# A routed two-block kernel: the search for the next expert visits TensorE at other places among the current expert's products

## The chip, the cores and the metric

One core of one Trainium2 chip. The metric is the device time of the whole kernel in microseconds. Three runs of the kernel before gave 707.58 us as median (704.78 to 709.69), and its profiled execution has a span of 709.6 us.

## What is computed

Two blocks follow each other. The first is linear attention with a norm: for every batch and head `kv = k^T v`, `out = q kv`, divided by its root mean square and scaled by `g_norm`. The second routes the 4608 tokens (512 wide) to 8 experts, 576 tokens each, and applies the expert's two-layer network:

```python
logits = x @ w_gate                       # 4608 x 8
order = np.argsort(-logits.flatten())
for idx in order:                         # the highest logit first
    tok, e = idx // E, idx % E
    if assigned[tok] >= 0 or counts[e] >= cap: continue
    assigned[tok] = e; counts[e] += 1
for e in range(E):
    h = np.maximum(x[assigned == e] @ w1[e], 0.0)    # 512 -> 1024
    out[assigned == e] = h @ w2[e]                   # 1024 -> 512
```

The greedy loop fills the experts one after the other. The kernel finds which expert fills next, and with which tokens, by a search for a threshold among the logits; expert t of the kernel, counted from 0 to 7, is the one that fills as number t.

## The kernel before

**Stages.** The attention takes the first part of the span and leaves its result in DRAM (`x_dram`). Then the first expert's tokens are searched with nothing beside it, and from 180.3 us on the eight experts' products run on TensorE one expert after the other, the last ending at 699 us. While expert t is multiplied, the search for a later expert is woven in between.

**One expert's products** (`layers`, L763). 64 fp32 matmuls of the first layer (`h_ps`, L798), then 56 of the second layer in seven products of eight (`y_ps`, L847; a Strassen-like scheme whose operand sums `tw` L779 and `sh` L789 GpSimd makes), then 8 for the last 64 tokens (L858). I call the place after k of these 128 matmuls "place k of expert t". VectorE makes six additions of these products (L818) and a last one for the 64 tokens (L866).

**One search** (`control`, L703) is a chain that goes to and fro between TensorE and VectorE. I name it after the expert it finds: search 1 to search 7, the last of which has no counting to do (`rest`, L598).

- seven counting steps (`threshold`, L468): TensorE counts with nine small matmuls (`n_ps`, L478) how many tokens lie over each of 32 candidate thresholds; VectorE finds the interval (L484 to L524), makes 32 new candidates (L271) and compares all tokens with them (`over`, L266), which the next count reads. The first count reads an `over` made right after the choice.
- the assignment (`assign`, L533): VectorE makes `sums` (L551), TensorE adds them up over the partitions (`all_ps`, L555), VectorE works out which tokens are taken. `here` (L561, L563) is part of it.
- the list (`fetch`, L627): VectorE makes `along` (L640), TensorE `a_ps` (L643), VectorE `since` (L652), TensorE `s_ps` (L656), and VectorE the row numbers `ids` (L668) with which GpSimd gathers the tokens from DRAM in five indirect transfers (`xg`, L673). VectorE then makes the output rows (L688 to L699).
- the choice (`choice`, L238): VectorE finds every token's best expert among those still open (L245 to L259), as the start of the next search.

**The turn** (`turn`, L723): VectorE scales the gathered tokens (`xs`, L733), TensorE transposes them (`t_ps`, L747), ScalarE writes `xt`, the next expert's input.

**What sets the order.** TensorE, VectorE and ScalarE run in the order in which the code records their instructions; GpSimd's is fixed too (`in_order`, L614). A search is a generator: each `yield` gives the time, in nominal microseconds of products, that TensorE is to spend on products before the search's next part is recorded. `layers` yields the nominal time of every matmul (0.487, 0.38, 0.858 for a pair), the main loop subtracts it, and when the wait is used up the next part is recorded there:

```python
                    wait -= used
                    while wait <= 0 and search():
                        pass
```

The number thus does not make an engine wait; it sets how many matmuls stand in TensorE's queue between one visit and the next. If VectorE is not ready when TensorE reaches the visit, TensorE stands still. Three other things steer the order: `search()` (L884) stops when two experts' weights are asked for ahead; at the first of the places marked `None` in `layers` (L839) a list that is still missing is recorded at once; and the turn begins 5.0 nominal microseconds (`hold`) after the list is recorded, its transposes standing at the marked places.

Of the kernel before, what the change touches and what calls it, by code (L numbers as in the profile page):

```python
# [25 lines left out]
def kernel(  # L26
# [16 lines left out]
    E, _, F = moe_w1.shape  # L43
# [93 lines left out]
    def small(nm, w=1, dt=FT):  # L137
        return asg.tile([P, w], dt, name=nm, tag="s_" + nm, bufs=2)
# [99 lines left out]
    def choice(c0=None, c1=GC):  # L238


        cs = slice(c0 or 0, c1)
        n = cs.stop - cs.start
        m, cm, cd = (mx, code_mx, code) if c0 is not None else (small_ps[k] for k in ("mx", "code_mx", "code"))
        if c0 is None:
            nc.vector.tensor_tensor(wl, lg, bc_e(small_ps["shut"]), op=AL.add)  # L245
        else:
            nc.vector.tensor_scalar(lg[:, :, cs], in0=lg[:, :, cs], scalar1=bound, scalar2=bottom,
                                    op0=AL.min, op1=AL.max)
        w = wl if c0 is None else lg
        nc.vector.tensor_reduce(m[:, cs], w[:, :, cs].rearrange("p e c -> p c e"), axis=AXX, op=AL.max)  # L250
        yield
        nc.vector.tensor_tensor(pick[:, :, cs], w[:, :, cs], bc_c(m[:, cs]), op=AL.is_ge)
        nc.vector.tensor_tensor(pick[:, :, cs], pick[:, :, cs], bc_e(cd, n), op=AL.mult)
        yield
        nc.vector.tensor_reduce(cm[:, cs], pick[:, :, cs].rearrange("p e c -> p c e"), axis=AXX, op=AL.max)
        yield
        nc.vector.tensor_tensor(best[:, :, cs], pick[:, :, cs], bc_c(cm[:, cs]), op=AL.is_equal)
        if c0 is None:
            nc.vector.tensor_tensor(mx, m, gone, op=AL.add)  # L259
# [5 lines left out]
    def compare(over, cand, c0=0, c1=GC):  # L265
        nc.vector.tensor_tensor(  # L266
            over[:, c0:c1], mx[:, c0:c1].rearrange("p (c o) -> p c o", o=1).to_broadcast([P, c1 - c0, NCAND]),
            cand[:, 1:NCAND + 1].rearrange("p (o n) -> p o n", o=1).to_broadcast([P, c1 - c0, NCAND]), op=AL.is_ge)

    def candidates(s, lo, cand):  # L270
        nc.vector.tensor_scalar(cand, in0=away[:, s], scalar1=lo, scalar2=None, op0=AL.add)  # L271
        return cand
# [170 lines left out]
    def bank(shape, nm):  # L443
        return psm.tile(shape, FT, name=nm, tag="c", bufs=1)
# [15 lines left out]
    def pieces():  # L460

        turn_of[0] += 1
        sm = small_ps["step"][:, turn_of[0] % 2]
        return sm[:, 0:2], sm[:, 2:]
# [3 lines left out]
    def threshold(t, over):  # L468

        lo, hi = bottom, top  # L470
        first, cand = t == 0, cand0
        for s in range(NSTEP):
            yield 4.6 if s > 0 else 0.4 if first else 2.0 if t == 1 else 4.0


            n_ps = bank([P, E, G], "n_ps")
            for c in range(0, GC, G):
                nc.tensor.matmul(n_ps, lhsT=over[:, c:c + G].rearrange("p c n -> p (c n)"),  # L478
                                 rhs=best[:, :, c:c + G],
                                 start=(c == 0), stop=(c == GC - G))  # L480
            need = goal[0:QP]
            for g in range(1, G):
                less = small("need", E)[0:QP]
                nc.vector.tensor_tensor(less, need, n_ps[g * QP:(g + 1) * QP, :, g], op=AL.subtract)  # L484
                need = less
            full = small("full", E)[0:QP]
            n_full = small("n_full")[0:QP]
            nc.vector.scalar_tensor_tensor(full, in0=n_ps[0:QP, :, 0], scalar=0.0, in1=need, op0=AL.add,
                                           op1=AL.is_ge, accum_out=n_full)
            if s + 1 < NSTEP:  # L490
                over = asg.tile([P, GC, NCAND], BF, name="over", tag="over", bufs=2)
            if first:
                ends = small("ends", 2)
                hi, lo = ends[:, 0:1], ends[:, 1:2]

                def pick_end(n):
                    at = small("at", NCAND + 1)
                    nc.vector.scalar_tensor_tensor(at, in0=row_f[:, 0:NCAND + 1], scalar=k_ps, in1=cand[:, n:NCAND + 1 + n],
                                                   op0=AL.is_equal, op1=AL.mult, accum_out=ends[:, 1 - n:2 - n])

                some = small("some_b", dt=BF)[0:QP]
                nc.vector.tensor_scalar(some, in0=n_full, scalar1=0.5, scalar2=None, op0=AL.is_gt)
                k_ps = psm.tile([P, 1], FT, name="k_ps", tag="h")
                nc.tensor.matmul(k_ps, lhsT=ones_b[0:QP, :], rhs=some, start=True, stop=True)
                pick_end(0)
                if s + 1 < NSTEP:
                    cand_next = small("cand", NCAND + 2)
                    compare(over, candidates(s + 1, lo, cand_next[:, 0:NCAND + 1]))
                pick_end(1)
                if s + 1 < NSTEP:  # L510
                    nc.vector.tensor_copy(cand_next[:, NCAND + 1:NCAND + 2], hi)
                    cand = cand_next
            else:

                some, some_t, kk = (small_ps[k][0:QP] for k in ("some", "some_t", "kk"))
                nc.vector.tensor_scalar(some, in0=n_full.to_broadcast([QP, 2 * QP]), scalar1=0.5, scalar2=None, op0=AL.is_gt)
                nc.vector.transpose(some_t[:, :, 0:QP], some.rearrange("p (t n) -> p t n", t=2))
                nc.vector.reduce_sum(out=kk, in_=some_t, axis=AXX)  # L520

                lo_was, (ends, cand_ps) = lo, pieces()
                for g in range(G):
                    nc.vector.tensor_scalar(ends[g * QP:(g + 1) * QP], in0=kk, scalar1=width[0:QP, s:s + 1],  # L524
                                            scalar2=lo_was[0:QP], op0=AL.mult, op1=AL.add)
                lo = ends[:, 1:2]
                if s + 1 < NSTEP:
                    compare(over, candidates(s + 1, lo, cand_ps))
                hi_was, hi = hi, small("hi")
                nc.vector.tensor_tensor(hi, ends[:, 0:1], hi_was, op=AL.min)  # L530
        return hi, lo

    def assign(t, ends):  # L533
# [15 lines left out]
        sums = small("sums", 2 * E, BF)  # L549
        with nc.allow_low_precision("counts of up to GC are exact in bf16"):  # L550
            nc.vector.reduce_sum(out=sums, in_=two.rearrange("p t e c -> p (t e) c"), axis=AXX)  # L551
        yield 5.4

        all_ps = bank([P, 3, E], "all_ps")
        nc.tensor.matmul(all_ps[:, 0], lhsT=ones_b, rhs=sums[:, 0:E], start=True, stop=True)  # L555
# [42 lines left out]
    def rest():  # L598
        which = small_ps["which"]
        nc.vector.tensor_reduce(which, code_left, axis=AXX, op=AL.max)  # L600
        index = small("index", dt=I32)
        nc.vector.tensor_scalar(index, in0=which, scalar1=-1.0, scalar2=float(E), op0=AL.mult, op1=AL.add)
        mine = small_ps["mine"]
        nc.vector.scalar_tensor_tensor(mine, in0=mx, scalar=NONE / 2, in1=small_ps["code_mx"], op0=AL.is_ge, op1=AL.mult)
        nc.vector.tensor_tensor(who, who, mine, op=AL.max)
        return which, index, lambda: None
# [20 lines left out]
    def fetch(t, which, index):  # L627
# [10 lines left out]
        nc.vector.tensor_scalar(own, in0=who, scalar1=which, scalar2=None, op0=AL.is_equal)  # L638
        along = small("along", GC, BF)
        nc.vector.tensor_tensor_scan(along, ones_b[:, 0:GC], own, 0.0, op0=AL.mult, op1=AL.add)  # L640
        yield 3.2 if t == 1 else 4.2 if t < E - 1 else 2.4
        a_ps = bank([P, GC + 1], "a_ps")
        nc.tensor.matmul(a_ps[:, 0:1], lhsT=before, rhs=along[:, GC - 1:GC], start=True, stop=True)  # L643
        nc.tensor.matmul(a_ps[:, 1:GC + 1], lhsT=fall, rhs=along, start=True, stop=True)
# [5 lines left out]
            nc.vector.tensor_scalar(since, in0=slot_f, scalar1=a_ps[:, 0:1], scalar2=None, op0=AL.is_ge)  # L650
        else:
            nc.vector.tensor_tensor(since, slot_f, a_ps[:, 0:1].to_broadcast([P, NB * P]), op=AL.is_ge)  # L652
        yield 1.6
        s_ps = bank([P, NB, GC + 3], "s_ps")
        for n in range(NB):
            nc.tensor.matmul(s_ps[:, n], lhsT=since[:, n * P:(n + 1) * P], rhs=kn, start=True, stop=True)  # L656
# [24 lines left out]
                              reason="TensorE waits for the tokens")  # L681
        if t > 0:
            yield "tokens"
            yield 1.5

        up = asg.tile([P, NB, 2, GC], FT, name="up", tag="up")
        for n in range(2):
# [15 lines left out]
    def control(t):  # L703

        if t < E - 1:
            which, index, later = yield from assign(t, (yield from threshold(t, compared.pop(t))))
        else:
            which, index, later = rest()
        if t > 0:
            yield "weights"  # L710
        yield from fetch(t, which, index)
        later()

        pause = None if t == 0 else 0.9
        if t + 1 < E:
            for _ in choice():
                yield pause
            yield pause
        if t + 1 < E - 1:
            compared[t + 1] = asg.tile([P, GC, NCAND], BF, name="over", tag="over", bufs=2)  # L720
            compare(compared[t + 1], candidates(0, bottom, pieces()[1]))
# [147 lines left out]
    with tc.manual_schedule(engines={PE, DVE, ACTE}):  # L869
# [3 lines left out]
        first = turn(0)  # L873
# [76 lines left out]
```

## Time and profile before

| what | value |
| --- | --- |
| device time, median of three | 707.58 us |
| TensorE busy, of the 709.6 us span | 616.8 us |
| VectorE busy | 443.3 us |
| GpSimd busy | 263.8 us |
| first expert's products begin, last expert's end | 180.3, 699 us |
| TensorE waiting for another engine between 205 us and the end | 9.3 us in 7 waits |

In a page of the profile, "busy" is the time an engine spent on instructions[...]. A row of the timeline gives the start, the time taken, the engine, the line, what is written from what, and in square brackets the idle time before it and the instruction whose end ended that idle time. A name such as `held_ps` stands for several small tiles that share one PSUM bank.

### The profile page before, as it was taken

How to read it: one execution, taken by the hardware profiler on the slowest of the kernel's cores; microseconds unless marked ns; L12 is line 12 of the kernel's file. 1: busy time of each engine (PE TensorE's matmuls, PEld its weight loads, DVE VectorE, ACT ScalarE, POOL GpSimd, SP SyncE). 2: the span in 40 equal slices, each digit the busy share in tenths (PEclk: the TensorE clock that was granted, in tenths of full speed). 3: DMA queues.
4: the chain of work that ended last, by engine and by line, in shares of the span. 5: the costliest groups of instructions: out<-in, count | busy, mean ns of one | idle time of the engine just before them, and what ended most of it. 6: DMA issues, size and time to landing. Idle time of an engine off the chain costs nothing.

```text
span 709.6 us, 13280 instructions
## 1 busy us (share of the span) xinstructions
PE 616.8 (87%) x5370; PEld 482.7 (68%) x5370; DVE 443.3 (62%) x1393; ACT 155.9 (22%) x315; POOL 263.8 (37%) x249
## 2 busy tenths in 40 slices
PE   3787788214999899989998999999899999999994
PEld 2566666212778677857885788678677867877782
DVE  4344656888687778888878779887887545020011
ACT  1454555300211121022102111121112022112100
POOL 0100011002342562438344632735263659226322
PEclk9988977555999999999999999999999999999998
DMA  8987889405303600531081053108013843001001
GB/s 283 316 278 237 278 297 351 177 0 184 129 1 103 251 26 1 205 137 38 6 306 67 1 180 132 68 1 312 28 41 127 293 165 106 0 30 38 0 1 67
DMA packets 41405, 93.41 MB, mean 132 GB/s; under 512 B 3456, under 2 KB 3456, under 8 KB 41344
## 3 DMA queue, kind: packets, MB, share of 16 engines
q1 hardware_dynamic: 34752, 72.49, 29.1%
q0 software_dynamic: 5888, 20.06, 8.1%
q8 instruction: 42, 0.69, 0.4%
q14 instruction: 19, 0.16, 0.1%
q10 hardware_dynamic: 704, 0.02, 0.1%
HBM read 72.50 MB, written 20.05 MB: 130 GB/s over the span
## 4 chain that ended last, share of the span: by engine, by line
PE 74%; DVE 13%; issue 6%; DMA 4%; ACT 1%; POOL 1%; POOLq 0%; ACTq 0%; DVEq 0%
PE h_ps L798 35%; PE y_ps L847 20%; PE o_ps L370 3%; PE qt_ps L301 3%; PE y_ps L858 3%; PE kv_ps L313 3%; PE t_ps L747 2%; DVE over L266 2%; DMA xg<-x_dram,ids 2%; PE n_ps L478 2%; DVE xs L733 1%; DMA gw<-in_moe_w_gate_dram 1%; PE warm_ps L625 1%; DVE need L484 1%; DVE held_ps L524 1%
## 5 line engine op out<-in xcount | busy, mean ns | idle before, releaser
L798 PE MATMUL h_ps<-xt,w_sb 128*128 128x288 f32 x1024 | 260.1, 410 | 0.8 <-ACT xt L750 0.8
L798 PEld LDWEIGHTS h_ps<-xt,w_sb 128*128 128x128 f32 x1024 | 190.6, 190 | 55.4 <-issue 5.7
L801 ACT ACTIVATE hid<-h_ps 128x288 f32<-128x288 f32 x128 | 52.6, 411 | 208.1 <-PE h_ps L798 208.1
L847 PE MATMUL y_ps<-tw,sh 128*128 128x256 f32 x384 | 86.5, 380 | 0.0
L847 PEld LDWEIGHTS y_ps<-tw,sh 128*128 128x128 f32 x384 | 72.0, 190 | 9.3
L789 POOL TENSOR_TENSOR sh<-hid 128x512 f32<-128x512 f32 x32 | 41.7, 1303 | 94.4 <-ACT hid L801 94.3
L673 POOL DMA_INDIRECT xg<-x_dram,ids x40 | 38.6, 964 | 82.8 <-DVE ids L668 35.8
L750 ACT ACTIVATE xt<-t_ps,g_col 128x512 f32<-128x512 f32 (+1 forms) x40 | 25.8, 645 | 161.6 <-PE t_ps L747 161.6
L847 PE MATMUL y_ps<-w_sb,hid 128*128 128x256 f32 x256 | 57.8, 381 | 0.0
L266 DVE TENSOR_TENSOR over<-mx,held_ps 128x1152 bf16<-128x1152 f32 x42 | 56.9, 1354 | 1.5
L818 DVE TENSOR_TENSOR y_sb<-y_ps,u 128x512 f32<-128x512 f32 x24 | 16.4, 684 | 63.8 <-PE y_ps L847 63.8
L756 POOL DMA_INDIRECT out_dram<-y_sb,outs x32 | 33.4, 1043 | 52.1 <-issue 36.7
L847 PEld LDWEIGHTS y_ps<-w_sb,hid 128*128 128x128 f32 x256 | 48.1, 190 | 6.6
L524 DVE TENSOR_SCALAR held_ps<-held_ps,width 32x2 f32<-32x2 f32 x144 | 41.3, 287 | 5.3
L779 POOL TENSOR_TENSOR tw<-w_sb 128x512 f32<-128x512 f32 x32 | 39.9, 1269 | 12.4 <-DMA w_sb<-in_moe_w_dram 12.3
L478 PEld LDWEIGHTS <-over 128*128 128x128 bf16 x441 | 17.5, 97 | 38.8 <-DVE over L266 27.5
L370 PE MATMUL o_ps<-kvx,qt 64*64 64x72 f32 x1152 | 32.9, 261 | 9.8 <-issue 9.2
L733 DVE TENSOR_TENSOR xs<-xg 128x512 f32<-128x512 f32 (+1 forms) x40 | 31.9, 809 | 14.7 <-DMA xg<-x_dram,ids 8.1
L478 PE MATMUL n_ps<-best,over 128*128 128x32 bf16 x441 | 19.3, 179 | 21.1 <-DVE over L266 19.2
L370 PEld LDWEIGHTS o_ps<-kvx,qt 64*64 64x64 f32 x1152 | 26.8, 160 | 15.5 <-issue 14.1
L378 DVE TENSOR_REDUCE ms<-sq 128x8 f32<-128x512 f32 x36 | 24.1, 681 | 20.1 <-ACT sq L376 19.9
L327 POOL COPY kvx<-kv 64x512 f32<-64x512 f32 x16 | 9.8, 609 | 71.3 <-DVE kv L321 70.9
(203 smaller groups left out, 831.9 us busy)
## 6 DMA issues: line engine op xcount, KB each, us to landing
w_sb<-in_moe_w_dram SPq DMA_DIRECT2D x16, 1024.0 KB, 6.3
w_sb<-in_moe_w_dram SPq DMA_DIRECT2D x8, 2048.0 KB, 13.3
k_sb<-in_k_dram SPq DMA_DIRECT2D x16, 576.0 KB, 5.4
v_sb<-in_v_dram SPq DMA_DIRECT2D x16, 576.0 KB, 5.8
q_sb<-in_q_dram SPq DMA_DIRECT2D x16, 576.0 KB, 5.6
x_dram<-o_sb SPq DMA_DIRECT2D x16, 576.0 KB, 4.3
x_dram<-o_sb SPq DMA_DIRECT2D x4, 288.0 KB, 4.2
xg<-x_dram,ids POOLq DMA_INDIRECT x40, 5.4
```

The source lines that it names most:

```text
L266: nc.vector.tensor_tensor(over[:, c0:c1], mx[:, c0:c1].rearrange("p (c o) -> p c o", o=1).to_broadcast([P, c1 - c0, NCAND]), cand[:, 1:NCA ...
L370: nc.tensor.matmul(o_ps[n * HP:(n + 1) * HP, rp, (2 * r2 + l) * W:(2 * r2 + l + 1) * W], lhsT=turned_q[bn][ks, block // 2, l * HP:(l + 1) ...
L478: nc.tensor.matmul(n_ps, lhsT=over[:, c:c + G].rearrange("p c n -> p (c n)"), rhs=best[:, :, c:c + G], start=(c == 0), stop=(c == GC - G))
L524: nc.vector.tensor_scalar(ends[g * QP:(g + 1) * QP], in0=kk, scalar1=width[0:QP, s:s + 1], scalar2=lo_was[0:QP], op0=AL.mult, op1=AL.add)
L673: tokens = nc.gpsimd.indirect_dma_start(out=xg[0:nr].rearrange("p h w -> p (h w)"), out_offset=None, in_=x_dram, in_offset=bass.IndirectOf ...
L733: nc.vector.tensor_tensor(xs[0:nr].rearrange("p (h d) -> p h d", h=H), xg[0:nr, :, 0:D], xg[0:nr, :, D:D + 1].to_broadcast([nr, H, D]), op ...
L756: put = nc.gpsimd.indirect_dma_start(out=out, out_offset=bass.IndirectOffsetOnAxis(ap=ids_of[t][0:nr, n:n + 1], axis=0), in_=y_sb[0:nr, :] ...
L779: in_order(nc.gpsimd.tensor_tensor(o[:, m:m + 2], x[:, m:m + 2], y[:, m:m + 2], op=AL.subtract))
L789: in_order(nc.gpsimd.tensor_tensor(o[:, ms], x[:, ms], y[:, ms], op=op))
L798: nc.tensor.matmul(h_ps, lhsT=w1[:, 2 * (d % 2) + d // 2, f * P:(f + 1) * P], rhs=xt[:, d, cs], start=(d == 0), stop=(d == DC - 1))
L801: nc.scalar.activation(hid[:, f, cs], h_ps, ACT.Relu)
L847: nc.tensor.matmul(p_ps[:, n], lhsT=left[:, f, n * P:(n + 1) * P], rhs=right[:, f], start=(f == 0), stop=(f == FH - 1))
```

## The change

Eight numbers of the order change, in six places; no instruction is added or removed. The visits of the first count, the list and the choice are put nearer to the visit before them, so that a search runs through fewer of the products and its list is made earlier. What the numbers belong to: the wait before the first count (search 1: 2.0 to 0.4, later ones: 4.0 to 3.4), before the sums of search 1 (5.4 to 5.0), before `a_ps` (3.2 to 1.8 and 4.2 to 2.6), before `s_ps` (1.6 to 1.1), before the output rows (1.5 to 0.7), and before each of the four parts of the choice (0.9 to 0.5).

```diff
@@ threshold
-            yield 4.6 if s > 0 else 0.4 if first else 2.0 if t == 1 else 4.0
+            yield 4.6 if s > 0 else 0.4 if t < 2 else 3.4
@@ assign
-        yield 5.4
+        yield 5.0 if t == 1 else 5.4
@@ fetch
-        yield 3.2 if t == 1 else 4.2 if t < E - 1 else 2.4
+        yield 1.8 if t == 1 else 2.6 if t < E - 1 else 2.4
@@ fetch
-        yield 1.6
+        yield 1.1
@@ fetch
             yield "tokens"
-            yield 1.5
+            yield 0.7
@@ control
-        pause = None if t == 0 else 0.9
+        pause = None if t == 0 else 0.5
```

## The prediction, made before the run

> **What bounds the kernel now.** I read the page first, then who TensorE waited for, then the timelines of TensorE, VectorE and GpSimd. The page:
>
> ```profile
> PE 616.8 (87%) x5370; PEld 482.7 (68%) x5370; DVE 443.3 (62%) x1393; ACT 155.9 (22%) x315; POOL 263.8 (37%) x249
> PE   3787788214999899989998999999899999999994
> DVE  4344656888687778888878779887887545020011
> ```
>
> From slice 11 (180 us) on TensorE is at nine tenths: the experts' products bound the span. But VectorE stands at seven to nine tenths until slice 31, because the search runs on it: it has little room there. Who TensorE waits for from 205 us to the end:
>
> ```profile
> PE t_ps L747 <- DVE xs L733: 8.7, 5, 2.3
> PE n_ps L478 <- DVE over L266: 0.6, 2, 0.4
> ```
>
> 9.3 us in all. That is the ceiling of any gain from moving visits: nothing else on TensorE changes. One counting step, on TensorE and on VectorE:
>
> ```profile
> 401.76 0.38 PE L478 MATMUL n_ps<-best,over 128*128 128x32 bf16 x9
> 401.99 5.10 PE L798 MATMUL h_ps<-xt,w_sb 128*128 128x288 f32 x20
> 406.92 0.38 PE L478 MATMUL n_ps<-best,over 128*128 128x32 bf16 x9
> ```
>
> ```profile
> 402.18 0.15 DVE L484 TENSOR_TENSOR need<-goal,n_ps 32x8 f32<-32x8 f32 x1 [0.59 <-PE n_ps L478]
> ...
> 405.33 1.35 DVE L266 TENSOR_TENSOR over<-mx,held_ps 128x1152 bf16<-128x1152 f32 x1
> ```
>
> TensorE comes back after 406.92-401.76 = 5.16 us. The next `over` is ready at 405.33+1.35+0.05 = 406.73 (0.05 us is the lag in the row where TensorE did wait, at 454.13). A step thus takes VectorE 4.97 us and leaves 0.2 us, less than one addition (L818, 0.60 from start to next start) or one scaled token block (L733, 0.61). From a list to the first count:
>
> ```profile
> 359.68 0.16 DVE L661 TENSOR_TENSOR rel_s<-place_f,s_ps 128x5 f32<-128x5 f32 x1 [0.76 <-PE s_ps L656]
> ...
> 366.26 0.68 DVE L818 TENSOR_TENSOR u<-y_ps,u 128x512 f32<-128x512 f32 x1
> ...
> 367.32 1.28 DVE L733 TENSOR_TENSOR xs<-xg 128x512 f32<-128x512 f32 x2
> ...
> 368.80 1.35 DVE L266 TENSOR_TENSOR over<-mx,held_ps 128x1152 bf16<-128x1152 f32 x1
> ```
>
> `s_ps` started at 359.35 and `over` ended at 370.15; less one addition (0.60) and two scaled blocks (1.20), the stretch takes VectorE 9.0 us with nothing between. And one row of what GpSimd can do to VectorE:
>
> ```profile
> 585.14 6.48 DVE L688 TENSOR_TENSOR up<-less,rise 128x180 f32<-128x180 f32 x2
> ```
>
> ```profile
> 583.70 2.48 POOL L779 TENSOR_TENSOR tw<-w_sb,tw 128x512 f32<-128x512 f32 x2
> 586.15 2.49 POOL L779 TENSOR_TENSOR tw<-w_sb 128x512 f32<-128x512 f32 x2
> 588.61 2.48 POOL L779 TENSOR_TENSOR tw<-tw,w_sb 128x512 f32<-128x512 f32 x2
> ```
>
> The same L688 pair takes 0.66 elsewhere; here it ends only when GpSimd's eight subtractions do.
>
> [...]6.48 against 0.66 us above; L561 1.25 against 0.75 and L563 1.34 against 0.46 in the one search (at 286 us) in which they met L789. L688, L561, L563 and L733 read two SBUF tiles; the counting steps read PSUM and show no such stretch. [...]
>
> **The change, part by part.** The work is the same; only distances change. I count matmuls in the order in which both programs issue them, with the trace's spacings: `h_ps` 0.487 (31.14 us for 64), `y_ps` 0.432, the last eight 0.468, four transposes 0.436, a count with the change of type 0.30 us.
>
> *What goes.* The lists stand earlier: list 1 at place 86 of expert 0 (was 98), list 2 at place 65 of expert 1 (was 92), lists 3 to 6 at 49, 36, 22, 10 (were 85, 77, 70, 63). The turns keep their places 109 to 124. In the trace list 2 was read at 296 us and its first scaled block, at 304 us, held TensorE for 2.35 us. With 12 to 60 more places between them, waits for tokens at the turn go. I book all 9.3 us as saved.
>
> *What comes: VectorE's queue.* From a list to the next first count TensorE now has 8.4 to 8.8 us (was 11.9 to 14.7), VectorE needs 9.0. Then steps of 4.97 us against 5.17 in the first layer and 5.9 in the products, where the six additions (3.6 us), five blocks (3.05) and the last part (0.65) have to pass too. Before, the choice and first count lay in that half and the steps in the first layer; now the steps lie in the products. For each search, at the place that binds, from the list on:
>
> - search 2: at expert 0's last transpose (place 124) TensorE is there after 19.1 us (34 x 0.432 + 4 x 0.468 + 4 transposes 1.74 + 2 counts 0.6 + 0.2); VectorE has 9.0 + 2 steps 9.94 + 4 additions 2.4 + 5 blocks 3.05 = 24.4. Wait 5.3.
> - search 3: place 118 of expert 1: TensorE 25.3; VectorE 9.0 + 14.9 + 4 blocks 2.44 + 3 additions 1.8 = 28.1. Wait 2.8.
> - search 4: place 115 of expert 2: 31.6 against 9.0 + 19.9 + 1.8 + 1.8 = 32.5. Wait 0.9.
> - search 5: place 124 of expert 3: 43.4 against 9.0 + 29.8 + 3.05 + 3.6 = 45.5. Wait 2.1.
> - search 6: place 115 of expert 4: 45.6 against 9.0 + 29.8 + 1.8 + 1.8 + sums 6.0 = 48.4. Wait 2.8.
>
> Sum 13.9 us. The first count of search 1 moves to place 1 of expert 0, 180.8 us; its `over` ended at 180.7: nothing. The list's other waits (`a_ps` to `s_ps` 1.5 against 1.3 us) fit. The wait before search 1's `a_ps` (4.1 us against 4.3) costs 0.2.
>
> *What comes: tokens behind GpSimd.* The first two blocks of a turn now stand right behind the first `over` on VectorE, 9.0 us after the list, and the second count's `over` is behind them. A gather lands 6.2 to 7.0 us after GpSimd starts it (424.95 to 431.69 in the trace, 6.7), the second starts 1.27 later, the first 1.8 after the list. Free, the second block lands 9.8 us after the list: hardly a wait. But list 2 at place 65 falls as GpSimd begins its second set of `sh` (at 284.07 to 289.8 us in expert 1): the gathers wait some 5.5 us, the second block is scaled at 13.9 instead of 10.2: 3.7. List 4, some 18.5 us into expert 3, falls into the first set (17.3 to 22.3 us after that expert's start): GpSimd is free 3.8 instead of 1.8 after the list: 2.0. List 5, 11.2 us into expert 4, falls into `tw` (4.7 to 14.5 us there, some 1 us earlier with the part before it): 0.5. Sum 6.2.
>
> [...] L561 of search 1 meets `sh` (its end at 220.1, the scan near 218.7): 1.4. In search 3 it meets `sh` as in the row of 1.25 and 1.34: 1.4, less 0.3 that is free. In search 4 it meets `tw`: 1.8 less 0.3. L688 of list 5 meets `tw`: 0 to 2.5. Bounds 0 and 6.5; half of it, 3.3, as two of the four meetings hang on a microsecond.
>
> Sum: 13.9 + 0.2 + 6.2 + 3.3 - 9.3 = +14.3 us, 707.6 + 14.3 = 722.
>
> **The rivals.**
> - *The waits just go.* If VectorE keeps up, 9.3 us of idle go and about 2 come back as the first counts' lack (9.0 against 8.4 to 8.8): 700. For it: all tokens are earlier, and TensorE bounds. Against it: 0.2 us of room per step. Chance 0.10.
> - *Only VectorE's queue.* [...]13.9 - 9.3, 712. For it: a gather free of GpSimd lands just in time. Against: the places of lists 2 and 4. Chance 0.20.
> - [...] All meetings cost their upper bound (3.2 more) and one lasts as long as the one at 585 us (5.8 more): 722 + 9 = 731. For it: that row. Against: L733 and L563 got in between two `sh`. Chance 0.15.
> - *The forecast*, 722: 0.55.
>
> **How the numbers follow.** The likeliest is 722. The range leaves out most of the first rival and the end of the third: 709 to 731. Slower by over 1% means above 714.7: the forecast almost whole, the third rival, and a third of the second: 0.74. Faster by over 1%, below 700.5: 0.07, most of the first. The rest, 0.19, is within.
>
> **What would show it.** Right: TensorE's waits after 205 us sum to some 20 to 28 us, most on `n_ps <- over` and on `t_ps <- xs` at places 118 and 124, none on tokens that are still in flight at the transposes; VectorE waits for `xg` in expert 1; L688 or L561 stretched beside L779 or L789. Wrong: fewer than 10 us of waits, or turns that still wait for the gather.

## The result and the profile after

The changed kernel takes 734.29 us (median of four runs, 733.58 to 738.3) against 708.63 us of the kernel before (704.78 to 713.57): a ratio of 1.037, interval 1.030 to 1.043, some 26 us slower. The forecast was 722 with a range to 731; the direction was right, the size too small.

The page of the changed kernel, the rows that answer to those of before (busy time of the engines, then VectorE in 40 slices of 18.4 us):

```profile
PE 625.8 (85%) x5370; PEld 487.5 (66%) x5370; DVE 459.3 (62%) x1393; ACT 156.0 (21%) x315; POOL 265.3 (36%) x249
DVE  4344556888789888888888888788867036020011
```

With the same instructions VectorE is busy 16 us longer (of the slices 12 to 29 all but two show an eight) and TensorE 9 us longer: part of the loss is not idle time at all but instructions that take longer. An instruction that is held up after its start counts as busy (L688 at 481.72 us below: 3.02 us busy, 0.66 elsewhere). The waits of TensorE from 205 us to the end (us in total, times, longest):

```profile
PE t_ps L747 <- DVE xs L733: 10.5, 6, 2.9
PE n_ps L478 <- DVE over L266: 10.5, 8, 3.4
PE a_ps L643 <- DVE along L640: 4.3, 3, 1.5
```

Before there were 8.7 and 0.6 us in the first two of these rows and nothing in the third. The waits of the turns, which earlier lists were to end, are still there; first counts and `a_ps` have been added.

As a measure for all kernels I take the stretch from the first `h_ps` to the last `y_ps` of the experts, called "the products" below, and TensorE's busy time in it. For before and after, a view of the trace by stretches gives start and end, length, busy time with its instructions, granted clock, DMA share and GB/s:

```profile
180.39:699.38 518.99, 509.58 (x2647) 1.00 0.27 97
```

```profile
184.71:726.27 541.56, 515.77 (x2647) 0.99 0.27 93
```

The products became 22.6 us longer: 16.4 us of idle time (9.4 to 25.8) and 6.2 us of busy time. The products began 4.3 us later in this profile of the changed kernel than in that of before; what runs ahead of them is the same in both. Over the 14 profiles of this study the start lay anywhere between 177.2 and 185.8 us, so I count the start as no part of the change. What the interval of the ratio (21.5 to 30.7 us) holds beyond 22.6 us I can't assign.

**Where the idle time lies.** By place, the waits of the changed kernel (25.7 us in all):

| search | `a_ps` | counts | turn |
| --- | --- | --- | --- |
| 1 | 1.27 | 0.41 | |
| 2 | | 0.75 | 1.51 + 1.87 |
| 3 | 1.45 | 3.16 | 1.81 |
| 4 | 1.53 | 0.39 + 0.81 | 0.61 |
| 5 | | 1.14 + 0.43 | 1.80 |
| 6 | | 3.39 + 0.44 | 2.92 |

The waits at the turns are VectorE's queue. The timeline of VectorE at search 2, and TensorE's row for the last transposes of that turn, each with the time that it takes after the start ("..." stands for rows left out):

```profile
248.35 1.28 DVE L733 TENSOR_TENSOR xs<-xg 128x512 f32<-128x512 f32 x2
249.67 0.15 DVE L484 TENSOR_TENSOR need<-goal,n_ps 32x8 f32<-32x8 f32 x1
...
252.82 1.35 DVE L266 TENSOR_TENSOR over<-mx,held_ps 128x1152 bf16<-128x1152 f32 x1
...
254.16 0.67 DVE L733 TENSOR_TENSOR xs<-xg 64x512 f32<-64x512 f32 x1
```

```profile
254.98 0.43 PE L747 MATMUL t_ps<-ident,xs 64*128 64x64 f32 x4 [1.87 <-DVE xs L733]
```

No row of VectorE here, nor of those left out, has a bracket: it never stood idle, the tokens were there. A whole counting step stands ahead of the last scaled block, and TensorE waits for that block.

The two long waits at first counts have another cause. List 2 of the changed kernel, VectorE and then GpSimd:

```profile
292.37 1.66 DVE L688 TENSOR_TENSOR up<-less,rise 128x180 f32<-128x180 f32 x2
...
294.63 0.57 DVE L693 TENSOR_SCALAR half<-at_row 128x5 f32<-128x5 f32 x1
295.23 1.18 DVE L694 TENSOR_TENSOR half<-half,got 128x5 f32<-128x5 f32 x1
...
301.27 1.35 DVE L266 TENSOR_TENSOR over<-mx,held_ps 128x1152 bf16<-128x1152 f32 x1
302.55 1.28 DVE L733 TENSOR_TENSOR xs<-xg 128x512 f32<-128x512 f32 x2
```

```profile
292.55 1.28 POOL L789 TENSOR_TENSOR sh<-sh,hid 128x512 f32<-128x512 f32 x1
293.80 1.37 POOL L789 TENSOR_TENSOR sh<-hid 128x512 f32<-128x512 f32 x1
295.13 1.27 POOL L789 TENSOR_TENSOR sh<-hid,sh 128x512 f32<-128x512 f32 x1
296.55 0.99 POOL L673 DMA_INDIRECT xg<-x_dram,ids  x1 [0.15 <-DVE half L694]
```

L688 takes 1.66 instead of 0.66, L693 and L694 0.57 and 1.18 where they take 0.17, each until a sum of GpSimd ends or just beyond. (L688 and L694 read two SBUF tiles; L693 reads one and writes one, and is held all the same.) The way from list to first count grows from 9.0 to 11.7 us, and TensorE waits 3.16 us. List 5 meets the differences `tw` in the same way: its L688 takes 3.02 us, the count after it waits 3.39.

```profile
481.72 3.02 DVE L688 TENSOR_TENSOR up<-less,rise 128x180 f32<-128x180 f32 x2
```

Behind both stand the gathers, delayed as well (296.55 here). By the time VectorE comes to the first scaled blocks (302.55), the tokens have landed.

The waits at `a_ps` end a chain that begins with `here` (L561, L563). At search 4, VectorE and then TensorE:

```profile
409.55 2.71 DVE L561 TENSOR_TENSOR_SCAN here<-inner,two 128x288 f32<-128x288 bf16 x1
```

```profile
416.05 0.16 PE L643 MATMUL a_ps<-along,before 128*128 128x1 bf16 x1 [1.53 <-DVE along L640]
```

L561 takes 0.75 us where GpSimd is at rest; here `tw` runs until 411.64. At searches 1 and 3 the two lines together take 2.37 and 3.08 us beside `sh` in place of 1.21. At searches 2, 5 and 6 neither is stretched, and `a_ps` is not waited for. No run takes this stretch away, so the link is read from these meetings alone.

**Where the busy time lies.** In stretches of 5 us, the last but two columns being the granted clock:

```profile
302.20:307.20 5.00, 4.52 (x22) 0.66 0.33 111
464.70:469.70 5.00, 4.71 (x23) 0.67 0.28 105
492.20:497.20 5.00, 4.90 (x21) 0.66 0.04 11
534.70:539.70 5.00, 4.85 (x20) 0.66 0.16 56
```

All four follow a wait of 1.8 to 3.4 us; about a third of some 19 us of busy time, 6.4 us, went to the lower clock. The 0.66 is a mean: in steps of 0.25 us the clock stands at 0.50 for 3.4 us in each of them and at 1.00 before and after. The kernel before has one such stretch, behind its wait of 2.32 us, at a cost of 1.6 us with the 2 us that follow it (the second row, behind a wait of 2.35, has none):

```profile
237.90:242.90 5.00, 3.59 (x14) 0.70 0.48 176
305.90:310.90 5.00, 5.00 (x30) 1.00 0.15 45
```

The difference, 4.8 us, is most of the 6.2 by which TensorE's busy time grew. In the second profile of the kernel before (below) it is the other way round: the wait of 2.33 us at search 2 has no such stretch behind it, that of 2.35 us at search 3 has one (0.74 and 0.58 in the two steps of 2.5 us from 302.42 us on). So the length of a wait alone does not tell whether the clock will fall.

### The profile page after: what moved, and what is told of

Read it like the earlier page. It is cut to its first block, busy times and chain, and to the rows that moved or that the text cites. A ratio compares the mean times of both kernels' runs of the same rounds, so it can differ in the third digit from the quotient of the medians.

```text
span 736.5 us, 13282 instructions
## 1 busy us (share of the span) xinstructions
PE 625.8 (85%) x5370; PEld 487.5 (66%) x5370; DVE 459.3 (62%) x1393; ACT 156.0 (21%) x315; POOL 265.3 (36%) x249
## 5 line engine op out<-in xcount | busy, mean ns | idle before, releaser
L818 DVE TENSOR_TENSOR y_sb<-y_ps,u 128x512 f32<-128x512 f32 x24 | 16.4, 683 | 84.8 <-PE y_ps L847 84.8
L750 ACT ACTIVATE xt<-t_ps,g_col 128x512 f32<-128x512 f32 (+1 forms) x40 | 25.8, 645 | 163.5 <-PE t_ps L747 120.9
L825 POOL TENSOR_TENSOR y_sb<-u,u 128x512 f32<-128x512 f32 x8 | 10.5, 1309 | 101.9 <-DVE u L818 101.9
L779 POOL TENSOR_TENSOR tw<-w_sb 128x512 f32<-128x512 f32 x32 | 39.9, 1268 | 12.4 <-DMA w_sb<-in_moe_w_dram 12.2
L370 PE MATMUL o_ps<-kvx,qt 64*64 64x72 f32 x1152 | 34.5, 270 | 6.5 <-issue 5.7
L313 PE MATMUL kv_ps<-v_sb,k_sb 64*64 64x64 f32 x1152 | 29.1, 248 | 10.8 <-issue 10.8
L301 PE MATMUL qt_ps<-ident,q_sb 128*128 128x128 f32 x144 | 32.1, 354 | 6.3 <-issue 1.9
```

The lines of the kernel that those rows point to most:

```text
L370: nc.tensor.matmul(o_ps[n * HP:(n + 1) * HP, rp, (2 * r2 + l) * W:(2 * r2 + l + 1) * W], lhsT=turned_q[bn][ks, block // 2, l * HP:(l + 1) ...
L779: in_order(nc.gpsimd.tensor_tensor(o[:, m:m + 2], x[:, m:m + 2], y[:, m:m + 2], op=AL.subtract))
```

## The experiments

| kernel | products | busy | idle | ratio to before (interval) |
| --- | --- | --- | --- | --- |
| before, two profiles | 519.0, 521.2 | 509.6, 509.9 | 9.4, 11.3 | |
| changed | 541.6 | 515.8 | 25.8 | 1.037 (1.030 to 1.043) |
| list alone | 528.9 | 513.3 | 15.6 | 1.012 (1.006 to 1.018) |
| choice and first count | 540.7 | 516.0 | 24.7 | 1.029 (1.021 to 1.037) |
| choice alone | 525.0 | 510.6 | 14.4 | 1.009 (1.006 to 1.012) |
| first count alone | 527.6 | 512.1 | 15.6 | 1.015 (1.010 to 1.020) |
| changed, longer steps | 534.4 | 512.0 | 22.3 | 1.022 (1.017 to 1.028) |
| changed, `rise` in PSUM | 542.3 | 517.1 | 25.2 | 1.032 (1.025 to 1.038) |
| changed, turn later | 543.7 | 516.5 | 27.2 | 1.030 (1.022 to 1.037) |
| changed, both of these | 534.5 | 512.0 | 22.5 | 1.016 (1.009 to 1.022) |
| changed, additions on ScalarE | 536.4 | 513.8 | 22.6 | 1.023 (1.016 to 1.030) |
| changed, two waits filled | 540.8 | 518.0 | 22.8 | 1.032 (1.025 to 1.038) |
| before, list early, counts in place | 513.2 | 507.7 | 5.5 | 0.990 (0.986 to 0.993) |

The second profile of before was the control:

> The kernel before once more, unchanged: how far its profile repeats. All theories: products of 518 to 520 us as in the first profile (519.0), idle time there of 9 to 10 us in the same waits; the start of the products, which no kernel here changes, anywhere between 177 and 186 us, as it lay in the profiles so far.

It gave 521.2 us of products: 2.2 us from the first profile, a little over what was expected, as one turn waited another 1.54 us. Differences of the products of 2 us and less are read from single waits below, not from the sum.

### One part of the change at a time

The list alone:

```diff
-        yield 3.2 if t == 1 else 4.2 if t < E - 1 else 2.4
+        yield 1.8 if t == 1 else 2.6 if t < E - 1 else 2.4
...
-        yield 1.6
+        yield 1.1
```

> Only the two waits inside the list are shortened (before a_ps 3.2/4.2 to 1.8/2.6, before s_ps 1.6 to 1.1); first count, output rows and choice keep their places. Lists 2 to 6 then stand at places 78, 65, 55, 46 and 35 or so, and TensorE has 10.3 to 13.2 us from a list to the next first count against the 9.0 that VectorE needs. Theory 1 (the queue on VectorE: too little room from list to first count, and steps that stand in the product half): the first counts find their candidates, about 1 us of waits on n_ps in all; the turns at places 118 to 124 wait as in the changed kernel but less; 6 to 11 us of waits in the experts' products, whose length is 519 to 523 us, a ratio of 1.00 to 1.01. Rival[...]: the lists meet GpSimd's sums too, L688 and L561 stretch by 1 to 3 us each, TensorE waits 15 us and more, products of 530 us, ratio 1.02.

528.9 us, between the two theories. The waits at the turns did shrink, to 3.8 us in all, but first counts waited 8.3 us, the longest 3.85, and `a_ps` 3.1 us in two waits. At the longest wait the scaled blocks stand ahead of the first count's `over`, and it was their tokens that were late:

```profile
359.48 0.69 DVE L733 TENSOR_TENSOR xs<-xg 128x512 f32<-128x512 f32 x1 [1.66 <-DMA xg<-x_dram,ids]
...
362.29 1.35 DVE L266 TENSOR_TENSOR over<-mx,held_ps 128x1152 bf16<-128x1152 f32 x1
```

The gathers for them began at 353.41 us, when GpSimd's `sh` had ended. The list's own rows were stretched here as well, as the rival had it (the second instruction of L688 1.41 us in place of 0.33), but VectorE, done with them, still had to wait for the tokens. So "tokens behind GpSimd" exists; in the changed kernel it was not seen, because there the first count stands ahead of the blocks and the list's own instructions were late too.

The other part:

```diff
-            yield 4.6 if s > 0 else 0.4 if first else 2.0 if t == 1 else 4.0
+            yield 4.6 if s > 0 else 0.4 if t < 2 else 3.4
...
-            yield 1.5
+            yield 0.7
...
-        pause = None if t == 0 else 0.9
+        pause = None if t == 0 else 0.5
```

> Only the waits of the first count (2.0/4.0 to 0.4/3.4), the output rows (1.5 to 0.7) and the choice (0.9 to 0.5) are shortened; the list keeps its own. TensorE has 8.4 to 9.0 us from a list to the first count, as in the changed kernel, where VectorE needs 9.0. Theory 1 (VectorE's queue): most of the loss is here. First counts wait 0 to 0.8 us each and the turns at places 115 to 124 wait 1 to 4 us each: waits of 14 to 18 us in the products, whose length is 526 to 530 us; ratio 1.01 to 1.02. Theory 3[...]: a first count waits 3 us only where its list meets GpSimd's sums (lists at places 93, 77, 63, 53 and 44 here, those of expert 2 and 3 among the first-layer's end): one such wait at most, shown by a stretched L688. [...]

540.7 us: this part alone is as slow as the whole change, 10 us more than I expected. The cause is as foreseen, the size not. At search 2 the turn's third block stands behind a whole step (VectorE, then TensorE):

```profile
238.21 2.36 DVE L733 TENSOR_TENSOR xs<-xg 128x512 f32<-128x512 f32 x2
...
243.74 1.35 DVE L266 TENSOR_TENSOR over<-mx,held_ps 128x1152 bf16<-128x1152 f32 x1
...
246.27 1.28 DVE L733 TENSOR_TENSOR xs<-xg 128x512 f32<-128x512 f32 x2
```

```profile
241.18 1.03 PE L847 MATMUL y_ps<-w_sb,sh 128*128 128x256 f32 x4
247.10 1.09 PE L747 MATMUL t_ps<-ident,xs 128*128 128x128 f32 x4 [4.89 <-DVE xs L733]
247.98 1.91 PE L847 MATMUL y_ps<-w_sb,sh 128*128 128x256 f32 x4
```

TensorE waits 4.89 us, the longest wait of that kernel, and the last row shows the other price: four `y_ps` passes (the trace of the kernel before has 1024 `h_ps` passes for 512 fp32 matmuls of the code, two for each) take 1.91 us there and 1.03 before the wait. Not all of the 24.7 us of idle time is VectorE's queue: one wait, 3.12 us at search 6, is for `a_ps`.

Its two halves (the first line of the diff above, then the other two):

> Of the part with choice and first count, only the wait before the first count is shortened (2.0/4.0 to 0.4/3.4). TensorE then has 11.0 to 11.9 us from a list to the next first count, lists 2 to 6 at places 93, 83, 75, 66, 59. Theory of the room (a first count and the blocks behind it wait only where TensorE gives VectorE less than the 9.0 us it needs plus the additions and blocks that stand between, 1 to 3 us): hardly a wait at first counts, turns as in the kernel before or 1 to 2 us more each: idle time 9 to 14 us, products of 520 to 526 us. Rival (every move of counts into the product half costs its share): half of the 21.8 us of the two moves together, products of about 530 us.

> Only the waits before the output rows (1.5 to 0.7) and before each part of the choice (0.9 to 0.5) are shortened. TensorE has 9.3 to 10.6 us from a list to the next first count; lists 2 to 6 at places 98, 85, 72, 60, 51. Theory of the room: the first counts wait up to 1 us (9.3 against 9.0 and one or two additions), the turns 1 to 3 us each: idle time of 13 to 18 us, products of 525 to 531 us, more than with the first count alone. Rival (shares that add up): 530 us, and together with the first count's part 540.7.

527.6 and 525.0 us; against the mean of the two profiles of before (520.1) they cost 7.5 and 4.9 us, together 12.4, where both at once cost 20.6. I had expected the first count to cost less than the choice; it cost more, with 15.6 us of idle time above the forecast's 14. One of its waits shows that room alone does not decide: ahead of the first count of search 5 (2.57 us) list 4 fell beside `sh`, and L688 took 2.55 us. That the halves do not add up fits the room (both at once leave 8.4 to 9.0 us for a way of 9.0), though no run tests this; and neither do the list's 8.8 and the others' 20.6 add up to the whole change's 21.5. Single waits can be explained; sums of parts can't be used.

### More room for a counting step

```diff
-            yield 4.6 if s > 0 else 0.4 if t < 2 else 3.4
+            yield 5.4 if s > 0 else 0.4 if t < 2 else 3.4
```

> The changed kernel with the wait between counting steps at 5.4 in place of 4.6: TensorE comes back after 5.9 to 6.0 us in the first layer in place of 5.16, so a step leaves VectorE 0.9 us, enough for an addition or a scaled block. The list to first count distance stays at 8.4 to 9.7 us. Theory 1 (steps with too little room): the waits of the turns and of second counts go, 25.8 us of idle time in the products fall to 10 or less; products of 524 to 530 us in place of 541.5, ratio to the kernel before of 1.01 and to the changed one of 0.98. Theory 3[...]: lists 2 to 5 stand at places 94, 88, 80, 73, beside other GpSimd work than in the changed kernel, and the two 3 us waits at first counts go with it, those at the turns stay: idle time of 17 to 20 us.

534.4 us, a gain of 7.2, and neither theory's number: the waits of the counts fell from 10.5 to 4.2 us (from 205 us on), but those of the turns rose from 10.5 to 15.4: idle time 22.3, not 10 or less, nor 17 to 20. Longer steps bring the list late again (place 101 of expert 0), the turn's first place comes 13 matmuls after it, and the blocks stand behind choice, `over` and three additions:

```profile
241.87 1.35 DVE L266 TENSOR_TENSOR over<-mx,held_ps 128x1152 bf16<-128x1152 f32 x1
...
244.34 1.28 DVE L733 TENSOR_TENSOR xs<-xg 128x512 f32<-128x512 f32 x2
```

```profile
245.07 1.12 PE L747 MATMUL t_ps<-ident,xs 128*128 128x128 f32 x4 [5.57 <-DVE xs L733]
```

So the step's lack of room was part of the loss. The rest fits a first count brought up close behind the list, wherever the list stands, but this run does not isolate it.

### The stretched rows and the tokens: one hides the other

```diff
-                      ("own", (GC,)),
+                      ("rise", (2, GC)), ("half", (NB,)),
...
+    nc.vector.tensor_copy(small_ps["rise"], rise)
...
-            nc.vector.tensor_tensor(up[:, :, n], less, rise[:, n].rearrange(
+            nc.vector.tensor_tensor(up[:, :, n], less, small_ps["rise"][:, n].rearrange(
```

`own` shares the bytes of `mine`; `half` lies in PSUM likewise; line numbers grow by one.

> The changed kernel, but `rise` and `half` lie in PSUM, so that the output rows (L688, L693, L694) no longer read two SBUF tiles. Nothing moves in TensorE's order. Theory 3[...]: the first counts of searches 3 and 6 wait 0.5 us or less in place of 3.16 and 3.39, L688 takes 0.7 us at every list, idle time falls from 25.8 to about 20 us and the slow clock after these two waits (about 1.5 us each) goes as well: products of 533 to 536 us, 6 to 8 us less than in the changed kernel. Theory 1 alone (VectorE's queue is too long whatever GpSimd does): the time saved there is waited at the turns instead; products of 540 us. Theory 2 (tokens behind GpSimd's sums hold the counts): no change either, the waits of 3 us stay and stand at xs waiting for xg.

Nothing was gained (542.3 us), although the stretch is gone: the two L689 take 0.58 us at list 2 (beside `sh`) and at list 5 (beside `tw`). What the chain won, VectorE spent on waiting for the tokens:

```profile
297.04 1.35 DVE L266 TENSOR_TENSOR over<-mx,held_ps 128x1152 bf16<-128x1152 f32 x1
300.00 1.44 DVE L734 TENSOR_TENSOR xs<-xg 128x512 f32<-128x512 f32 x2 [1.61 <-DMA xg<-x_dram,ids]
```

```profile
298.45 0.39 PE L479 MATMUL n_ps<-best,over 128*128 128x32 bf16 x9 [1.29 <-DVE over L266]
...
306.62 0.39 PE L479 MATMUL n_ps<-best,over 128*128 128x32 bf16 x9 [2.07 <-DVE over L266]
```

1.29 + 2.07 = 3.36 us in two counts where 3.16 stood in one; at search 6 it is 0.92 + 3.13 where 3.39 + 0.44 stood. The blocks wait (VectorE's waits for `xg` from 205 us on grow from 2.6 to 8.7 us, 4.1 of it before 500 us, where the changed kernel has none), and the second count's `over` waits behind them. The reverse, with the turn later and the stretch left in:

```diff
-            hold, turning = 5.0, None
+            hold, turning = 12.0, None
```

> The changed kernel with the turn begun 12 in place of 5 nominal microseconds after the list, so that the scaled blocks stand later in VectorE's queue; TensorE's order stays the same. With the run that took `rise` to PSUM two readings are left for the 3.2 and 3.4 us waits at the first counts of searches 3 and 6. Theory A (two hidden stretches in parallel, the stretched output rows and the scaled blocks that wait for tokens behind GpSimd's sums; taking away one leaves the other): here the output rows stay stretched, so the first counts of searches 3 and 6 still wait about 3 us, idle time 24 to 26 us, products 540 to 543 us. Theory B (the scaled blocks alone hold the counts): both waits fall under 1 us, idle time about 20 us, products 534 to 536 us.

543.7 us: no gain either, the first counts of searches 3 and 6 waited 3.16 and 4.10. And both at once:

> The changed kernel with both: `rise` and `half` in PSUM (no stretched output rows) and the turn begun 12 nominal microseconds after the list (no scaled block waiting for its tokens ahead of a count). Theory A (the two hide each other): now the waits of searches 3 and 6 in the first half of the products go, some 6 us with 1 to 3 us of slow clock behind them: idle time 18 to 20 us, products 533 to 536 us in place of 541.5. Theory 1 alone (VectorE's queue is too long in any case, the time is only waited at the turns instead): products of 539 us or more, the turns waiting longer by what the counts gain.

534.5 us, 7 us less than the changed kernel, though each alone gave nothing: two delays side by side, of which each hides the other. At the first two counts TensorE waited (us):

| search | changed | `rise` in PSUM | turn later | both |
| --- | --- | --- | --- | --- |
| 3 | 3.16 | 3.36 | 3.16 | 1.28 |
| 6 | 3.83 | 4.05 | 4.10 | 3.05 |

The length came out as theory A had it, its parts did not: idle time fell only to 22.5, as search 2's turn waited 3.41 us and the first count of search 6 still 2.35; the rest of the gain is 3.8 us less busy time (one stretch of low clock, in steps of 2.5 us some 6.8 us long and at 0.50 throughout 247.4 to 252.4 us, in place of four of 3.4). The count of search 6 shows where a taken-away stretch goes. Of the list's instructions one still reads two SBUF tiles, and now it is the one that waits for `tw` to end:

```profile
477.46 0.58 DVE L689 TENSOR_TENSOR up<-less,held_ps 128x180 f32<-128x180 f32 x2
...
479.33 1.94 DVE L700 SCALAR_TENSOR_TENSOR code_left<-code,held_ps,code_left 128x8 f32<-128x8 f32 x1
```

### Less work in VectorE's queue

```diff
-            add(quarter(0, 0), p_ps, u1)
+            nc.scalar.copy(quarter(0, 0), p_ps)
...
-            add(u3, p_ps, u2)
+            nc.scalar.copy(u3, p_ps)
```

and the other four additions likewise: the kernel leaves out the second operand of each of the six sums, so it shows the time without VectorE's additions and does not compute the network.

> The changed kernel, but the six VectorE additions of every expert's second layer are copies of the product by ScalarE: the second operand of each sum is left out. This takes 6 x 0.60 = 3.6 us per expert off VectorE's queue, where the steps of the search stand among them, and moves nothing on TensorE. Theory 1 (VectorE's queue in the product half): the waits at turns and counts from place 84 on lose 1.8 to 3.0 us each where they last so long: search 2 about 4.1 to 1.7, search 3's 1.8 to 0, search 4's 0.6 to 0, search 5's 1.8 to 0, search 6's 2.9 to 1; idle time of 17 to 19 us, products of 532 to 535 us. The waits of 3.2 and 3.4 us at the first counts of searches 3 and 6 stay (they lie in GpSimd's sums), so do those of a_ps. Rival (the turns wait for tokens, not for VectorE's queue): idle time 24 us and more, products of 540 us.

536.4 us, 5 us gained where 7 to 10 were forecast. The turns' waits fell where additions stood ahead of the block: search 2's 1.51 and search 5's 1.80 went, search 3's 1.81 became 1.00. Search 6's stayed (2.81 after 2.92): ahead of that block stands the assignment's beginning, not an addition. And the count of search 5 went from 1.14 to 2.75, since TensorE and VectorE now came to list 4 earlier and its L688 met more of `sh` (2.55 us; 1.08 in the changed kernel); in the same way the first count of search 6 went from 3.39 to 4.32. List 4's row:

```profile
415.36 2.55 DVE L688 TENSOR_TENSOR up<-less,rise 128x180 f32<-128x180 f32 x2
```

### The slow clock behind a wait

```diff
+            if s == 0 and t in (3, 6):
+                w_ps = bank([P, 512], "warm_ps")
+                for _ in range(12):
+                    nc.tensor.matmul(w_ps, lhsT=ones_b, rhs=wide, start=True, stop=True)
             n_ps = bank([P, E, G], "n_ps")
```

> The changed kernel with twelve bf16 matmuls 128x512 that nothing reads before the first count of searches 3 and 6, some 2.6 us of TensorE work each, in the place where it waited 3.16 and 3.39 us: TensorE comes to these counts when their candidates are nearly ready, having worked instead of waited. Clock theory (the slow matmuls behind a long wait are the price of the wait itself: the 20 passes behind the wait of search 6 took 6.79 us instead of 5.10): they run at full clock behind these two counts, products shorter by 1.5 to 3 us, 538.5 to 540 us. Rival (the clock falls for another reason[...]): products of 541.5 us or more, and the passes still slow.

The passes behind both counts ran at full clock, as the clock theory has it: 1.00 in the 5 us from 298.50 and from 487.20 us, where the changed kernel has 0.66 in the 5 us from 302.20 and from 492.20. The products behind the first count of search 6, in the changed kernel and with the wait filled (the same 20 passes; line numbers grow by four):

```profile
492.30 0.39 PE L478 MATMUL n_ps<-best,over 128*128 128x32 bf16 x9 [3.39 <-DVE over L266]
492.54 6.79 PE L798 MATMUL h_ps<-xt,w_sb 128*128 128x288 f32 x20
```

```profile
487.51 5.10 PE L802 MATMUL h_ps<-xt,w_sb 128*128 128x288 f32 x20
494.69 0.39 PE L482 MATMUL n_ps<-best,over 128*128 128x32 bf16 x9 [2.08 <-DVE hi L534]
```

6.79 against 5.10 us. At search 3, eight `y_ps` passes take 1.97 instead of 3.46. (The busy 518.0 us of this kernel in the table include the 24 matmuls that fill, 5.5 us.) But the products shrank by 0.8 us, less than the 1.5 forecast: the last row shows it. TensorE came to the next count earlier, VectorE was no earlier (7.42 us from first count to second, 7.46 in the changed kernel), and 2.08 us were waited there in place of 0.44; behind that wait the clock fell in its turn (0.50 in the 2.5 us from 495.52 us). So the slow matmuls between these two visits cost little (0.8 us of the products), where VectorE's chain is the bound. What they cost where TensorE is the bound, no run isolates.

### Early where it does no harm

The kernel before, with the list's waits of the change, and what this saves added to the wait before the next first count, so that all counts stay within one place of where they were:

```diff
-            yield 4.6 if s > 0 else 0.4 if first else 2.0 if t == 1 else 4.0
+            yield 4.6 if s > 0 else 0.4 if first else 2.0 if t == 1 else 6.9 if t == 2 else 6.5 if t < 5 else 6.1
...
-        yield 3.2 if t == 1 else 4.2 if t < E - 1 else 2.4
+        yield 1.8 if t == 1 else 2.6 if t < E - 1 else 2.4
...
-        yield 1.6
+        yield 1.1
```

> The kernel before with the list's own waits shortened as in the change, but the wait before the next first count lengthened (4.0 to 6.9, 6.5 and 6.1) so that all counts of the searches stay within one place of where they were: lists 1 to 5 stand at places 92, 85, 78, 70, 64 in place of 98, 92, 85, 77, 70, and only the tokens come earlier. Theory 1 (earlier is good where nothing of VectorE's counting moves; the loss of the change came from counts that stand in the product half with too little room): the turns of searches 2 and 3, which waited 2.32 and 2.35 us for tokens, wait under 0.5; those of searches 4 and 6 (1.83 and 1.86, behind a counting step) stay; idle time 4 to 6 us in place of 9.35, products of 513 to 517 us in place of 519, ratio 0.99 to 0.997. Rival (every earlier list meets GpSimd's sums): stretched output rows or scans, a_ps waits of 1.5 us at two or more searches, products of 520 us or more, ratio 1.00 or above.

704.47 us against 711.94, a ratio of 0.990 (0.986 to 0.993): a small gain, but faster than both kernels, products 513.2 us. The waits from 205 us on:

```profile
PE t_ps L747 <- DVE xs L733: 4.8, 4, 1.8
PE a_ps L643 <- DVE along L640: 0.5, 1, 0.5
PE n_ps L478 <- DVE over L266: 0.2, 1, 0.2
```

Search 2's turn waited 0.20 and 1.05 in place of 2.32, search 3's not at all in place of 2.35; 1.83 and 1.72 at searches 4 and 6 stayed. No stretch of the products, in steps of 2.5 us, shows a clock under 0.98, and TensorE's busy time fell by 1.9 us as well.

## Why the prediction fell short

- **The products' own time: the step that failed.** "... nothing else on TensorE changes", says the prediction. I counted every `h_ps` and `y_ps` at the trace's median spacing and took the sum as fixed. The changed kernel spent 6.2 us more on the same matmuls, 4.8 of it at the lower clock behind more of the long waits, which is in no term of my sum. The kernel before has the price in plain sight: the four `y_ps` passes behind its wait of 2.32 us take 1.85 us in place of 1.03.

```profile
239.31 0.66 PE L747 MATMUL t_ps<-ident,xs 128*128 128x128 f32 x4 [2.32 <-DVE xs L733]
239.81 1.85 PE L847 MATMUL y_ps<-w_sb,sh 128*128 128x256 f32 x4
```

In the changed kernel the clock stood at 0.50 for 3.4 us at a time, behind waits of 1.80, 2.92, 3.16 and 3.39 us. It did not fall behind 2.35 us in the kernel before, nor behind 2.9 us in the kernel with two waits filled.

- **VectorE's queue, 13.9 us.** Right in mechanism and nearly in size. Search 2: 5.3 forecast, 4.1 measured; search 3's turn 2.8 and 1.8; search 4 0.9 and 1.8; search 5 2.1 and 3.4; search 6's turn and second count 2.8 and 3.4: 14.5 in all, with some 0.4 us of a stretched L688 (1.08) in search 5's. The experiment with the additions shows it for searches 2, 3 and 5. The 0.41 us at search 1's first count I had put at nothing.
- **Tokens behind GpSimd, 6.2 us.** Not in the trace of after: VectorE waited 2.6 us for `xg`, all of it after 620 us and none in expert 1, and no first count for it. It was there as the second of two delays side by side, and I had priced it as one on its own. The 6.2 to 7.0 us from a gather's start to its landing are too narrow a reading as well: the 40 gathers of the kernel before take 3.3 to 7.0 us, 5.4 as median. (The gather given as 424.95 to 431.69 starts at 424.90, and its block at 431.64.) The 3.16 us at search 3 look like the 3.7 forecast, but the stretched rows caused them.
- **Meetings with GpSimd, 3.3 us (0 to 6.5).** Too small, and its upper bound as well. All four meetings came, where I had taken half: the scans of searches 1, 3 and 4 cost 1.27 + 1.45 + 1.53 = 4.3 us in waits on `a_ps`, and the first counts of searches 3 and 6, behind stretched output rows, another 6.6. List 2's meeting with `sh` I had not counted, nor any line behind L688. Beside `tw`, L688 stood until the last of the instructions that GpSimd had left (6.48 us in the kernel before, 3.02 at list 5 of the changed one), and where it is taken out the next row with two SBUF inputs stands in its place (L700, 1.94 us).
- **Saved, 9.3 us.** Right as arithmetic, since all waits of after were summed anew, but the reason was wrong. Only the 4.7 us of searches 2 and 3 had to do with tokens, and at search 3 not wholly: the block began at 304.22 us, as its tokens landed, and then took 1.57 us in place of 0.68, beside a GpSimd instruction (L825, 303.98 to 305.25). The waits of searches 4 to 6 (1.83, 0.36, 1.86) stand in VectorE's queue already in the kernel before; the first of them, on VectorE, right behind a counting step:

```profile
375.22 1.35 DVE L266 TENSOR_TENSOR over<-mx,held_ps 128x1152 bf16<-128x1152 f32 x1
...
376.56 0.68 DVE L733 TENSOR_TENSOR xs<-xg 128x512 f32<-128x512 f32 x1
```

An earlier list can't end such waits: in the kernel with the early list those of searches 4 and 6 stayed (1.83, 1.72), and only the 0.36 went.

- **The sum.** Waits: 23.6 gross forecast, 25.7 measured, two errors of the parts nearly cancelling, which is luck (meetings up by 7.5, tokens down by 6.2). Net +14.3 against +16.4. Missing are the 6.2 us of busy time; the base was 1 us higher in the runs beside it (708.63), and some 3 us of the median are not seen in the traced products. The range, to 731, held the meetings at their worst but no slower TensorE, so it ended too low.

## What to carry to other kernels

A visit should be moved only as far as the engine behind it has room: count what that engine needs from this visit to the next, with everything that stands in its queue between, and move what brings data (the list) apart from what starts the next chain (the count). Put a price on each long wait beyond its own length, since TensorE's granted clock stood at 0.50 for 3.4 us behind four of the changed kernel's. And of delays that run side by side and end at the same place take the longer, not the sum (here either one taken away gained nothing, both together 7 us): to prove one, take away both.

## What the runs showed of the hardware

- Beside `tw`, GpSimd's run of instructions held L688, which has two SBUF inputs, until the run's end (3.02 us at list 5, 6.48 in the kernel before at 585 us, 0.66 elsewhere); beside `sh`, L688, L693 and L694 went on when one of the sums ended or just beyond (1.66, then 0.57 and 1.18 us at list 2). Why the two differ stays open. With `rise` in PSUM the work of L688 took 0.58 us beside either. L693, a `tensor_scalar` that reads one SBUF tile and writes another, was held too (0.57 us for 0.17), and not beside `sh` where it wrote to PSUM (0.17).
- GpSimd's `sh` took longer too, 1.72 us in place of 1.27, where L563 or `xs` overlapped it.
- Behind waits of 1.80 to 3.39 us the granted clock of the changed kernel fell to 0.50 for 3.4 us, at a cost of 6.4 us in the four stretches together. It stayed at 1.00 behind others (1.81 and 1.87 us in the same kernel, 2.35 in the kernel before, 2.9 in the kernel with two waits filled). With `rise` in PSUM it stood at 0.50 throughout 495.70 to 500.70 us. With twelve bf16 matmuls (2.75 us) before the first count of search 3, and as many before that of search 6, it was 1.00 behind both counts.
